# Linear attention into a gated MLP on one core: batch 1's loads, norms and turn rearranged

## The chip, the cores and the metric

The kernel runs on one core of one Trainium2 chip. The metric is the time of one execution on the device in microseconds, as the median over several runs.

## What is computed

Attention without a score matrix: q is normed over the head dimension, k over the sequence, and a 64 x 64 product of k and v per head takes the place of the scores. Its output, 4608 tokens by 512, goes through an MLP with hidden width 2048 and the activation h * sigmoid(beta * h).

```python
q_s = exp(q - max(q, -1));  q_s = q_s / (sum(q_s, -1) + 1e-9)      # q, k, v: (8, 8, 576, 64)
k_s = exp(k - max(k, 2));   k_s = k_s / (sum(k_s, 2) + 1e-9)
kv  = einsum('bhsd,bhse->bhde', k_s, v)
x   = einsum('bhsd,bhde->bhse', q_s, kv).transpose(0, 2, 1, 3).reshape(4608, 512)
h   = x @ w_in                                                      # 512 -> 2048
out = (h * (1 / (1 + exp(-beta * h)))) @ w_out                      # 2048 -> 512
```

Inputs and output are float32; products run in bfloat16.

## The kernel before

**Tiling.** The tokens are cut into nine slabs of 512: slab t below 8 holds the first 512 positions of batch t, slab 8 the last 64 of each batch. A slab has two passes. Pass 1 makes the hidden layer transposed, 16 tiles of 128 hidden rows (`pass1_tile`, index f), each of four 128x128 by 128x512 products (index m, one for each pair of heads) into one PSUM bank, then one Silu on ACT into `GT` (L648). Pass 2 (`pass2_group`) multiplies `GT` by `WOUT` into four output tiles (index u) of 16 products each. A product of both passes is one 128x512 matmul; PE has one line for all of them, L372, and L370 for transposes.

**The attention part** works on pairs of heads (hp 0 to 3). `exp_q` (L314, ACT) makes `EQ` from `QF`. `norm_main` (L331) sums each row (L338, DVE), takes the reciprocal (L339, DVE) and multiplies (L340, on DVE or on GpSimd, named POOL). For batch 1, `t_steps` transposes the normed pairs on PE (L370) and copies them to `QT` (L391, ACT). `exp_kc` (L322, ACT) and `cast_v` (L357) prepare k and v; `kv_half` multiplies them for two pairs (36 small products) and scales the result into `KVC` (L441 and L443, DVE); `out_half` makes two pairs of `XT`, the input of pass 1, by four products of 64x64 by 64x512 and a copy from PSUM for each pair (`out_evac`, L459).

**The weights.** `load_wout` brings float32 rows of W_out into staging buffers, which are the ones that W_in came through: rows 8 to 11 go into `O2S[1]`, as soon as DVE has cast the W_in that lay there. `scale_wout` (L562, DVE) scales one row block f with 1/beta into `WOUT`. A product of pass 2 with index f needs row block f.

**What sets the order.** Each engine works through its own queue in the order in which the program adds the operations, and `add` derives the waits from what an operation reads and writes, PSUM banks included. All loads below are issued by SP, in program order. The order around the first turn, from slab 0 to slab 1, is written out by hand. In pass 2 of slab 0, f is the outer loop and all four u run side by side in banks 3 to 6; for f of 14 and 15, u = 0 and 1 come first. Before pass 2 stand, for DVE, `scale_wout` and the norms of batch 1 (L795 to L808). Inside it, `todo` (L756) inserts batch 1's work after given products: `slot` starts at 64, so an entry of 104 comes after product 40 of the 64. Bank numbers of slab 0's and slab 1's tiles come from `HFIRST` (L652); beyond its end, slab 1 takes banks 0, 1, 2 in turn. `FIRST` (L669) says how many tiles of a slab are begun at the turn, with the m loop outside, so that products with m = 0 and 1 can run before pairs 2 and 3 of `XT` are there (`by_m`, L657). `o2_evac` (L702) copies an output tile from PSUM to `O2S` for the store.

**Loads of batch 1's q.** `load_swapped` (L272) has four loads x of 256 KB, two heads each: x = 0 is pair 0, x = 1 is pair 2, and x = 2 and x = 3 are the even and the odd heads of pairs 1 and 3 together. So pairs 1 and 3 need both x = 2 and x = 3.

Of the kernel before, what the change touches and what calls it, by code (L numbers as in the profile page):

```python
# [7 lines left out]
ACT = mybir.ActivationFunctionType  # L8
# [35 lines left out]
class Program:  # L44
# [12 lines left out]
    def add(self, eng, fn, r=(), w=(), bank=(), slot=None, after=()):  # L57
        op = Op(eng, fn, slot)
        op.pos = len(self.ops)
        deps = op.deps  # L60
        deps.extend(after)
        for k in r:
            deps.extend(self.writer.get(k, ()))
            self.readers.setdefault(k, []).append(op)
        for k in w:
            for d in self.readers.get(k, ()):
                if d is not op and not self._same(d, op):
                    deps.append(d)
            for d in self.writer.get(k, ()):
                if not self._same(d, op):  # L70
                    deps.append(d)
            self.readers[k] = []
            self.writer[k] = [op]
        for k in bank:
            t = self.touch.setdefault(k, {})
            for e, d in t.items():
                if e != eng:
                    deps.append(d)
            t[eng] = op
        if eng == POOL and slot is None:  # L80
            if self.pool is not None:
                deps.append(self.pool)
            self.pool = op
        self.ops.append(op)
        return op
# [78 lines left out]
def bass_efficient_attn_shen__then__act_swish_beta_kernel(  # L164
# [12 lines left out]
    with ExitStack() as es:  # L177
# [36 lines left out]
        WARM = sb("WARM", [128, 512], BF16)  # L214
# [57 lines left out]
        def load_swapped(b, xs=range(4)):  # L272
            i = b % 2
            for x in xs:
                s0, d0, n = SLOTS[x]
                a = bass.AP(qt_h, (b * H + s0) * S * D,
                            [[4 * D, 128], [n * S * D, 2], [1, 4 * D]])
                o = bass.AP(QF[i], d0 * 4 * D, [[H * 4 * D, 128], [n * 4 * D, 2], [1, 4 * D]])
                add(SP, lambda e, o=o, a=a: e.dma_start(o, a),
                    w=[("qf", i, hp, x) for hp in ((0,), (2,), (1, 3), (1, 3))[x]],  # L280
                    slot=f"qs{i}{x}")
# [173 lines left out]
        def out_evac(b, bks, hps=range(NHP)):  # L455
            i = b % 2
            for hp in hps:
                eng, bk = (ACTE if hp % 2 else DVE), bks[hp]
                add(eng, lambda e, eng=eng, bk=bk, hp=hp: (  # L459
                    e.copy if eng == ACTE else e.tensor_copy)(XT[i][:, hp, :], PS[bk][:, :]),  # L460
                    r=[("ps", bk)], w=[("xt", i, hp)], bank=[bk])
# [19 lines left out]
        def kv_half(b, bks, a):  # L481
            kv_prods(b, bks, (a,))
            kv_evac(b, bks, (a,))

        def out_half(b, bks, a):
            out_prods(b, bks, (a,))
            out_evac(b, bks, (a, a + 1))
# [53 lines left out]
        def go(steps):  # L541
            for s in steps:
                s()
# [105 lines left out]
                                                 scale=BETA[:, f:f + 1]),  # L649
                    r=[("ps", bk), "beta"], w=[("gt", f)], bank=[bk])  # L650

        HFIRST = ((3, 4, 5, 6, 0, 1, 7, 2, 3, 4, 5, 6, 0, 1, 7, 2), (1, 3, 2, 4, 5, 6, 0, 7))  # L652

        def hbank(t, f):
            return HFIRST[t][f] if t < 2 and f < len(HFIRST[t]) else HB[f % 3]
# [10 lines left out]
                pass1_mm(t, f, m, bk)  # L666
                tick()

        FIRST = (16, 5)  # L669
        at = by_m(0, 0, 4)  # L670
        at(0)
        out_now(0, 3, 7, DVE)
# [14 lines left out]
                at(m)  # L687
        load_wout(0)
        load_wout(4)
        load_swapped(1, (0, 2))  # L690
        load_wout(8)
        load_swapped(1, (3, 1))
        load_k(1, 4, (0, 1))
        load_wout(12, 2)
        load_v(1, 4, (0, 1))
# [51 lines left out]
        for t in range(NSLAB):  # L747
            todo = []
            if t == 0:
                def evacs():  # L750
                    o2_evac(0, 0, 3, DVE)
                    o2_evac(0, 1, 4, ACTE)
                    add(ACTE, lambda e: e.activation(DUMMY[:, 2:3], WARM[:, 0:1], ACT.Silu),
                        r=["warm"], w=["dummy"])

                todo = [(104, lambda: go(t_steps(1, (0, 1), (1,), ACTE))),  # L756
                        (104.1, lambda: cast_v(1, 0, ACTE)),
                        (109, lambda: go(t_steps(1, (2, 3), (2,), ACTE))),
                        (109.1, lambda: (scale_wout(14, 2), exp_kc(1, 2), exp_kc(1, 3))),
                        (115, lambda: kv_half(1, (7, 0), 0)),  # L760
                        (122, lambda: out_half(1, (1, 2), 0)), (124.5, evacs),
                        (127, lambda: kv_half(1, (7, 0), 2))]
            elif t == 1:
                todo = [(103, lambda: (kv_prods(2, (1, 2), (0, 2)), kv_evac(2, (1, 2)))),
                        (118, lambda: block(2))]
            elif t < 7:
                todo = [(104, lambda: block(t + 1))]
            todo = sorted(todo, key=lambda x: -x[0])
            slot = [0]

            def tick():
                slot[0] += 1
                while todo and todo[-1][0] <= slot[0]:
                    todo.pop()[1]()

            if 2 <= t < 7:
                if t < 5:
                    load(t + 2 if t == 2 else t + 3)
                for hp in (0, 2):
                    norm_main(t + 1, hp, 2)  # L780
                    t_dma(t + 1, hp, 2)
                if t in (2, 3, 4, 6):
                    norm_rem(t // 2 if t != 3 else 0)
                    tr_dma(t // 2 if t != 3 else 0)
                if t == 2:
                    load(5)
            elif t == 1:
                for hp in range(NHP):
                    cast_v(2, hp)
            if t < 2:  # L790
                slot[0] = NM * FIRST[t]
            for f in range(FIRST[t] if t < 2 else 0, NF):
                pass1_tile(t, f, tick)
            if t == 0:
                load(2)  # L795
                scale_wout(0)
                scale_wout(4)
                exp_q(1, (0,))
                norm_main(1, 0, 1)
                scale_wout(8)  # L800
                exp_q(1, (1, 3, 2))
                norm_main(1, 1, 1, POOL)
                norm_main(1, 3, 1, POOL)
                norm_main(1, 2, 1)
                exp_kc(1, 0, 2)
                scale_wout(12, 2)
                for hp in range(1, NHP):
                    cast_v(1, hp)  # L808
                pass2_group(0, (0, 1, 2, 3), (3, 4, 5, 6), tick)
                while todo:  # L810
                    todo.pop()[1]()
                at = by_m(1, 0, FIRST[1])
                o2_evac(0, 2, 5, ACTE)
                at(0, 0, 3)
                at(1, 0, 3)
                out_half(1, (7, 7, 7, 0), 2)
                o2_evac(0, 3, 6, DVE)
                at(0, 3)
                at(1, 3)
                at(2)  # L820
                at(3)
                store(0)
                load(3)
                load_qrem(0)
                continue
            nb = [t + 2] if t + 2 < B else []
            if t == 1:
                nb = [2, 3]
            late = []
            for b in nb:  # L830
                if t == 1 and b == 2:
                    exp_q(2)
                    for hp in range(2):
                        norm_main(2, hp, 1, POOL)
                    t_dma(2, 0, 2)
                for hp in (0, 2):
                    exp_kc(b, hp, 2)
                if b > 2:
                    late.append(b)
                if b > 3:  # L840
                    for hp in range(NHP):
                        cast_v(b, hp)
            for b in late:
                exp_q(b)
                if b % 2 == 1:
                    exp_qr(b // 2)
                if b == 3:
                    exp_qr(0)
            for u in range(4):
                if (t, u) == (8, 3):  # L850
                    last_tile(u, ((0, 384), (384, 512)), (OB[orot[0] % 2], MB[0]))
                    continue
                pass2_group(t, (u,), (OB[orot[0] % 2],), tick)
                orot[0] += 1
                if t == 1 and u == 0:
                    for hp in range(2, 4):
                        norm_main(2, hp, 1, POOL if hp == 2 else DVE)
                    t_dma(2, 2, 2)
                    for hp in range(NHP):
                        cast_v(3, hp)  # L860
            while todo:
                todo.pop()[1]()
            if t < 8:
                store(t)
# [30 lines left out]
```

## Time and profile before

| | |
|---|---|
| median of 9 runs | 280.62 us (280.43 to 282.29) |
| the profiled execution | 280.53 us |
| its span, first to last instruction | 278.7 us |
| granted TensorE clock | 1.000 |
| PE busy in the span | 270.1 us (97%) |
| ACT, DVE, POOL busy | 166.8, 102.6, 33.5 us |
| a Silu (L648) | 689 ns, 144 of them |
| GpSimd's norm multiply (L340) of one pair | 1042 ns, 8 of them |
| pass 2 of slab 0 and the turn to slab 1 | about 28 to 48 us of the span |

Rows of a timeline read: start in us from the span's start, duration in us, engine, line of the kernel, operation, output tile <- input tiles, shape, how many merged; in brackets the idle time of the engine before the row and what ended it. PEld is the weight load of a matmul. A few per cent of the matmul records are missing, so a count of 5 may stand for 6. In a group line, the numbers after the bar are busy us and mean ns of one, then the idle time before.

### The profile page before, as it was taken

What the parts mean: (1) busy time and instruction counts of PE and PEld (TensorE: products, weight loads), DVE (VectorE), ACT (ScalarE), POOL (GpSimd) and SP (SyncE); (2) the same over time, 40 slices, a digit from 0 to 9 for tenths busy, and PEclk for the clock granted to TensorE, in tenths of its full rate; (3) what the DMA queues carried; (4) which work ended last, traced back from release to release, by engine and by line L of the source; (5) the groups of instructions that cost most, each with busy time, mean ns of one, the idle gap of its engine ahead of it and who ended that gap; (6) DMA issues with size and microseconds to landing.
All of it is one profiled execution on the core that took longest, in us unless ns stands there. A gap on an engine that the chain in (4) does not pass through costs nothing.

```text
span 278.7 us, 4595 instructions
## 1 busy us (share of the span) xinstructions
PE 270.1 (97%) x1899; PEld 131.0 (47%) x1929; DVE 102.6 (37%) x206; ACT 166.8 (60%) x240; POOL 33.5 (12%) x50
## 2 busy tenths in 40 slices
PE   7899989999999999999999999999999999999995
PEld 3545444444445454545454545444444444444443
DVE  4744785008590149205730462035603300110012
ACT  4868476889578736793579437853751175027500
POOL 2630041307000304030002000000000000000000
DMA  7999999997089799960599133002600120011022
GB/s 228 385 387 401 388 390 377 393 374 136 17 290 368 201 341 281 388 133 2 153 383 209 33 150 75 2 4 94 151 0 2 58 93 2 0 75 75 2 73 78
DMA packets 42174, 50.12 MB, mean 180 GB/s; under 512 B 21029, under 2 KB 29477, under 8 KB 41001
## 3 DMA queue, kind: packets, MB, share of 16 engines
q1 hardware_dynamic: 41312, 48.90, 54.3%
q10 hardware_dynamic: 840, 0.93, 1.1%
q8 instruction: 15, 0.25, 0.4%
q14 instruction: 7, 0.05, 0.0%
HBM read 36.71 MB, written 9.44 MB: 166 GB/s over the span
## 4 chain that ended last, share of the span: by engine, by line
PE 84%; DMA 8%; SPq 4%; DVE 2%; issue 1%
PE PS L372 84%; DMA O2S<-in_moe_w_out_dram 4%; DMA O2S<-in_moe_w_in_dram 4%; SPq L569 2%; SPq L250 1%; DVE QS L338 1%; DVE WOUT L562 1%; DVE EQ L340 0%; SPq L293 0%; DVE WIN L573 0%; PE PS L370 0%; DVE QI L339 0%; SPq L298 0%; DVE O2S L724 0%
## 5 line engine op out<-in xcount | busy, mean ns | idle before, releaser
L648 ACT ACTIVATE GT<-PS,BETA 128x512 bf16<-128x512 f32 x144 | 96.8, 689 | 61.6 <-PE PS L372 61.6
L372 PE MATMUL PS<-WOUT,GT 128*128 128x512 bf16 (+2 forms) x573 | 125.2, 373 | 1.8 <-issue 1.3
L372 PE MATMUL PS<-XT,WIN 128*128 128x512 bf16 x566 | 125.6, 379 | 0.8 <-issue 0.3
L372 PEld LDWEIGHTS PS<-XT,WIN 128*128 128x128 bf16 x576 | 60.4, 106 | 63.6 <-issue 0.4
L372 PEld LDWEIGHTS PS<-WOUT,GT 128*128 128x128 bf16 x592 | 56.6, 98 | 65.8 <-issue 1.1
L703 DVE COPY O2S<-PS 128x512 f32<-128x512 f32 x33 | 22.7, 688 | 124.3 <-PE PS L372 124.3
L357 POOL CAST VB<-VF 128x576 bf16<-128x576 f32 x29 | 21.2, 730 | 85.6 <-DMA VF<-in_v_dram 84.3
L338 DVE TENSOR_REDUCE QS<-EQ 128x8 f32<-128x512 bf16 (+1 forms) x22 | 20.0, 910 | 17.3 <-ACT EQ L314 17.3
L459 ACT CAST XT<-PS 128x512 bf16<-128x512 f32 x14 | 7.6, 587 | 23.2 <-PE PS L372 23.2
L322 ACT ACTIVATE EK<-KF 128x1152 bf16<-128x1152 f32 (+1 forms) x19 | 18.4, 1005 | 3.2 <-DMA KF<-in_k_dram 2.9
L314 ACT ACTIVATE EQ<-QF 128x512 bf16<-128x512 f32 x32 | 17.6, 615 | 4.3 <-DMA QF<-in_q_dram 4.3
L340 DVE TENSOR_TENSOR EQ<-EQ,QI 128x1024 bf16<-128x1024 bf16 (+1 forms) x14 | 16.2, 1156 | 0.5
L459 DVE CAST XT<-PS 128x512 bf16<-128x512 f32 x14 | 9.1, 686 | 13.4 <-PE PS L372 13.4
L340 POOL TENSOR_TENSOR EQ<-EQ,QI 128x512 bf16<-128x512 bf16 x8 | 8.3, 1042 | 32.8 <-DVE QI L339 32.4
L372 PEld LDWEIGHTS PS<-VB,EK 64*64 64x64 bf16 x576 | 6.6, 107 | 5.0 <-issue 2.5
L372 PE MATMUL PS<-VB,EK 64*64 64x65 bf16 x576 | 8.0, 193 | 0.8 <-ACT VB L357 0.4
L648 ACT ACT_TABLE_LOAD x5 | 6.4, 1283 | 0.1
L372 PE MATMUL PS<-QT,KVC 64*64 64x512 bf16 x64 | 6.2, 383 | 0.0
L372 PE MATMUL PS<-XT 128*128 128x512 f32 x6 | 4.4, 887 | 1.5 <-DVE XT L226 1.5
L339 DVE RECIPROCAL QI<-QS 128x8 f32<-128x8 f32 (+1 forms) x22 | 5.0, 226 | 0.8
L322 ACT ACT_TABLE_LOAD x4 | 5.1, 1283 | 0.1
L443 DVE TENSOR_TENSOR KVC<-PS,RC 128x128 bf16<-128x128 f32 (+1 forms) x16 | 4.4, 274 | 0.6
(51 smaller groups left out, 66.9 us busy)
## 6 DMA issues: line engine op xcount, KB each, us to landing
out_dram<-O2S SPq DMA_DIRECT2D x8, 1024.0 KB, 4.6
QF<-in_q_dram SPq DMA_DIRECT2D x30, 256.0 KB, 6.0
KF<-in_k_dram SPq DMA_DIRECT2D x6, 1152.0 KB, 8.4
VF<-in_v_dram SPq DMA_DIRECT2D x6, 1152.0 KB, 11.7
KF<-in_k_dram SPq DMA_DIRECT2D x8, 288.0 KB, 8.2
VF<-in_v_dram SPq DMA_DIRECT2D x8, 288.0 KB, 8.5
WST<-in_moe_w_in_dram SPq DMA_DIRECT2D x8, 256.0 KB, 7.4
O2S<-in_moe_w_in_dram SPq DMA_DIRECT2D x4, 512.0 KB, 10.8
```

The source lines that it names most:

```text
L314: add(ACTE, lambda e, o=o, a=a: e.activation(o, a, ACT.Exp), r=[("qf", i, hp, x) for x in ((2, 3) if hp % 2 else (hp // 2,))], w=[("eq", i ...
L322: add(ACTE, lambda e: e.activation(o, a, ACT.Exp), r=[("kf", i, h) for h in range(hp, hp + n)], w=[("ekc", i, h) for h in range(hp, hp + n)])
L338: add(DVE, lambda e: e.tensor_reduce(s_, a, AX.X, ALU.add), r=ks, w=[("qs", i, hp0)])
L339: add(DVE, lambda e: e.reciprocal(v_, s_), r=[("qs", i, hp0)], w=[("qi", i, hp0)])
L340: add(eng, lambda e: e.tensor_tensor(a, a, vb, ALU.mult), r=ks + [("qi", i, hp0)], w=ks)
L357: add(eng, lambda e: (e.copy if eng == ACTE else e.tensor_copy)(o, a), r=[("vf", i, hp), ("vone", i)], w=[("vb", i, hp, h) for h in ((0, 1 ...
L372: add(PE, lambda e: e.matmul(o, l, r_, start=start, stop=stop, tile_position=tp), r=r, w=w, bank=[bk])
L443: add(DVE, lambda e, o=o, p_=p_, vb=vb: e.tensor_tensor(o, p_, vb, ALU.mult), r=[("ps", bk)] + [("rc", i, hp) for hp in hps], w=[("kvc", k ...
L459: add(eng, lambda e, eng=eng, bk=bk, hp=hp: (e.copy if eng == ACTE else e.tensor_copy)(XT[i][:, hp, :], PS[bk][:, :]), r=[("ps", bk)], w=[ ...
L569: add(SP, lambda e: e.dma_start(STAGE[c][:, m:m + nm, :], a), w=SKEY[c][m:m + nm], slot=f"win{c}{m}")
L648: add(ACTE, lambda e: e.activation(GT[:, f, :], PS[bk][:, :], ACT.Silu, scale=BETA[:, f:f + 1]), r=[("ps", bk), "beta"], w=[("gt", f)], ba ...
L703: add(eng, lambda e: (e.copy if eng == ACTE else e.tensor_copy)(O2S[t % 2][:, u, :], PS[bk][:, :]), r=[("ps", bk)], w=[("o2", t % 2, u)], ...
```

## The change

All of it concerns batch 1 at the turn from slab 0 to slab 1:

- load x = 3 of batch 1's q is issued ahead of W_out rows 8 to 11, not behind them;
- the norm of pair 0 multiplies on GpSimd, not on DVE, and `scale_wout(8)` is cut in two: rows 8 and 9 before pair 1's norm, rows 10 and 11 after it;
- the entries of `todo` move: transposes of pairs 0 and 1 from after product 40 to after 42, of pairs 2 and 3 from 45 to 49, the first kv half from 51 to 53, the first output half from 58 to 59;
- the second kv half, which stood before product 64, stands behind six products of slab 1 (three tiles, m = 0 and 1); the second output half, which stood there, stands behind six more;
- slab 1 begins six tiles at the turn, not five, and takes all eight banks for its 16 tiles;
- the copy of output tile u = 3 and the activation that loads the Silu table are added before slab 1's first products; the table's load stands behind the copy of tile u = 2, not before it;
- in the second output half of batch 1, ACT copies pair 2 and DVE pair 3, where it was the other way round.

```diff
-                eng, bk = (ACTE if hp % 2 else DVE), bks[hp]
+                eng, bk = (ACTE if (hp % 2) != (b == 1 and hp > 1) else DVE), bks[hp]
...
-        HFIRST = ((3, 4, 5, 6, 0, 1, 7, 2, 3, 4, 5, 6, 0, 1, 7, 2), (1, 3, 2, 4, 5, 6, 0, 7))
+        HFIRST = ((3, 4, 5, 6, 0, 1, 7, 2, 3, 4, 5, 6, 0, 1, 7, 2), (1, 3, 2, 4, 5, 6, 7, 0, 1, 3, 2, 4, 5, 6, 7, 0))
...
-        FIRST = (16, 5)
+        FIRST = (16, 6)
...
-        load_swapped(1, (0, 2))
+        load_swapped(1, (0, 2, 3))
         load_wout(8)
-        load_swapped(1, (3, 1))
+        load_swapped(1, (1,))
...
                     o2_evac(0, 0, 3, DVE)
                     o2_evac(0, 1, 4, ACTE)
-                    add(ACTE, lambda e: e.activation(DUMMY[:, 2:3], WARM[:, 0:1], ACT.Silu),
-                        r=["warm"], w=["dummy"])
-
-                todo = [(104, lambda: go(t_steps(1, (0, 1), (1,), ACTE))),
-                        (104.1, lambda: cast_v(1, 0, ACTE)),
-                        (109, lambda: go(t_steps(1, (2, 3), (2,), ACTE))),
-                        (109.1, lambda: (scale_wout(14, 2), exp_kc(1, 2), exp_kc(1, 3))),
-                        (115, lambda: kv_half(1, (7, 0), 0)),
-                        (122, lambda: out_half(1, (1, 2), 0)), (124.5, evacs),
-                        (127, lambda: kv_half(1, (7, 0), 2))]
+
+                todo = [(106, lambda: go(t_steps(1, (0, 1), (1,), ACTE))),
+                        (106.1, lambda: cast_v(1, 0, ACTE)),
+                        (113, lambda: go(t_steps(1, (2, 3), (2,), ACTE))),
+                        (113.1, lambda: (scale_wout(14, 2), exp_kc(1, 2), exp_kc(1, 3))),
+                        (117, lambda: kv_half(1, (7, 0), 0)),
+                        (123, lambda: out_half(1, (1, 2), 0)), (124.5, evacs)]
...
-                norm_main(1, 0, 1)
-                scale_wout(8)
+                norm_main(1, 0, 1, POOL)
+                scale_wout(8, 2)
                 exp_q(1, (1, 3, 2))
                 norm_main(1, 1, 1, POOL)
+                scale_wout(10, 2)
                 norm_main(1, 3, 1, POOL)
                 norm_main(1, 2, 1)
...
                 o2_evac(0, 2, 5, ACTE)
+                o2_evac(0, 3, 6, DVE)
+                add(ACTE, lambda e: e.activation(DUMMY[:, 2:3], WARM[:, 0:1], ACT.Silu),
+                    r=["warm"], w=["dummy"])
                 at(0, 0, 3)
                 at(1, 0, 3)
-                out_half(1, (7, 7, 7, 0), 2)
-                o2_evac(0, 3, 6, DVE)
+                kv_half(1, (7, 0), 2)
                 at(0, 3)
                 at(1, 3)
+                out_half(1, (7, 7, 7, 0), 2)
                 at(2)
                 at(3)
```

## The prediction

> **What bounds the kernel now.** The page first: PE is busy for 97% of the span, and the chain of work that ended last is PE for 84%.
>
> ```profile
> PE 270.1 (97%) x1899; PEld 131.0 (47%) x1929; DVE 102.6 (37%) x206; ACT 166.8 (60%) x240; POOL 33.5 (12%) x50
> PE 84%; DMA 8%; SPq 4%; DVE 2%; issue 1%
> ```
>
> So the change pays only where PE waits, and whatever PE loses goes onto the end: in order of time the chain of waits is PE without a break from 39.27 us on, and its long pieces start at 226.07, 236.86, 247.66, 258.45 us, 50 products every 10.79 us (0.216 us each; one record in 50 is missing). Next, PE's timeline where slab 0 turns into slab 1:
>
> ```profile
> 36.80 0.39 PE L370 MATMUL PS<-IDB,EQ 128*128 128x128 bf16 x4
> 37.60 0.40 PE L370 MATMUL PS<-IDB,EQ 128*128 128x128 bf16 x4 [0.42 <-POOL EQ L340]
> 37.84 1.24 PE L372 MATMUL PS<-WOUT,GT 128*128 128x512 bf16 x5
> 39.27 0.62 PE L370 MATMUL PS<-IDB,EQ 128*128 128x128 bf16 x8 [0.19 <-DVE EQ L340]
> 39.73 1.46 PE L372 MATMUL PS<-WOUT,GT 128*128 128x512 bf16 x6
> ...
> 46.78 0.41 PE L372 MATMUL PS<-QT,KVC 64*64 64x512 bf16 x4
> 47.12 12.82 PE L372 MATMUL PS<-XT,WIN 128*128 128x512 bf16 x57
> ```
>
> See two waits. Pair 1's transposes could start at 37.02 and start at 37.60: 0.58 us. After five products (38.92) pairs 3 and 2 start at 39.27: 0.35. Two more are too short for these rows: in its single instructions, pair 3's share of the second kv half waits 0.09 us for GpSimd's cast, and at 53.7 us PE waits for a bank whose Silu was late (58 products from 47.12 to 59.78 are 12.66 us, 12.53 at the rate: 0.13). Together 1.15 us: all that can be won. Then DVE, which makes what PE waits for, and its neighbours:
>
> ```profile
> 32.36 0.69 DVE L340 TENSOR_TENSOR EQ<-EQ,QI 128x512 bf16<-128x512 bf16 x1
> 33.92 1.67 DVE L562 TENSOR_SCALAR WOUT<-O2S,RB 128x512 bf16<-128x512 f32 x4 [0.87 <-DMA O2S<-in_moe_w_out_dram]
> 35.51 0.68 DVE L338 TENSOR_REDUCE QS<-EQ 128x8 f32<-128x512 bf16 x1
> 36.22 0.20 DVE L339 RECIPROCAL QI<-QS 128x8 f32<-128x8 f32 x1
> 36.34 0.63 DVE L338 TENSOR_REDUCE QS<-EQ 128x8 f32<-128x512 bf16 x1
> ...
> 38.03 1.18 DVE L340 TENSOR_TENSOR EQ<-EQ,QI 128x512 bf16<-128x512 bf16 x1
> 39.14 0.87 DVE L562 TENSOR_SCALAR WOUT<-O2S,RB 128x512 bf16<-128x512 f32 x2
> 40.28 1.16 DVE L562 TENSOR_SCALAR WOUT<-O2S,RB 128x512 bf16<-128x512 f32 x2 [0.28 <-DMA O2S<-in_moe_w_out_dram]
> ```
> ```profile
> 36.50 2.16 POOL L340 TENSOR_TENSOR EQ<-EQ,QI 128x512 bf16<-128x512 bf16 x2 [19.30 <-DVE QI L339]
> 39.63 0.90 POOL L357 CAST VB<-VF 128x576 bf16<-128x576 f32 x1 [0.97 <-DMA VF<-in_v_dram]
> 42.50 0.67 POOL L357 CAST VB<-VF 128x576 bf16<-128x576 f32 x1 [1.97 <-DMA VF<-in_v_dram]
> ```
> ```profile
> 34.68 1.67 ACT L314 ACTIVATE EQ<-QF 128x512 bf16<-128x512 f32 x3 [3.32 <-DMA QF<-in_q_dram]
> 47.27 0.59 ACT L459 CAST XT<-PS 128x512 bf16<-128x512 f32 x1 [0.42 <-PE PS L372]
> ```
>
> From 33.92 to 39.14 DVE never rests: its start is the landing of W_out rows 8 to 11, its end is row 12's scaling. And DVE and GpSimd hinder each other. The multiply (L340) takes 0.69 us alone, 1.18 beside GpSimd's, ending (39.21) 0.55 after GpSimd's end (38.66). GpSimd's cast takes 0.67 alone and 0.90 where it starts during a scaling, ending (40.53) 0.52 after that scaling (40.01); the next scaling, started at 40.28, ends (40.81) 0.28 after the cast.
>
> [...] The trace agrees: the three endings above, and the reduces of 0.63 to 0.68 us beside GpSimd's multiply. [...] The trace agrees: the waits for loads end in the order of issue.
>
> **Part 1, one load sooner.** Load x=3 (odd heads of pairs 1 and 3) goes ahead of W_out 8. Before, W_out 8 was there for DVE at 33.92 and x=3 for ACT at 34.68, so x=3 takes about 0.70 us (256 KB at the 389 GB/s of that window are 0.67). W_out 8 was issued at 22.71 and landed 11 us later, behind a full queue; so it now lands 0.70 later, DVE starts row 8 at 34.62. SP has time for the issue (its wait before 22.71). ACT's exponentials of pairs 1 and 3 come 2.6 us sooner, hidden: DVE's reduces stand behind rows 8 and 9. Loads after x=3 land as before.
>
> **Part 2, the norms.** Pair 0's multiply goes to GpSimd at 32.4, done by 33.45, under free time. DVE is then at: row 8 34.62, row 9 35.02 (0.40 apart: 1.59 us for four), reduce of pair 1 35.42, reciprocal 36.13 (0.71), row 10 36.25 (0.12), to end at 36.73. GpSimd asks for pair 1's multiply at 36.41 (0.28 after the reciprocal's start, as at 36.22 and 36.50). [...] GpSimd, asking before row 11's start at 36.65, gets it: ends 36.73 + 0.90 (1.04[...]) = 37.63. Row 11 ends 0.28 later, 37.91. The reverse, [...] no row shows; row 11 would end at 37.13. [...] Then reduce of pair 3 37.83, reciprocal 38.54, reduce of pair 2 38.66, reciprocal 39.33 (0.67), multiply 39.57 (0.24). GpSimd's pair 3 runs 38.82 to 39.86, so DVE's multiply ends 0.55 later, 40.41. GpSimd's cast of pair 1's v (landed by 39.63) asks at 39.93, before row 12's start at 40.33, so it goes first, to 40.93, and row 12 ends at 41.21. Before: 39.61.
>
> **PE against it.** Before, product 40 starts at 36.58. Now 41 and 42 follow, at 0.1 us late for row 8, then the transposes of pairs 0 and 1, the latter at 37.69, done at 37.92, hidden by what follows; products 43 to 48 to 39.21. Product 49 needs row 12: 41.21 + 0.06 = 41.27, a wait of 2.06 us. Queued behind it are pairs 3 and 2's transposes and all of PE. Product 50 starts at 41.27 + 0.22 + 0.46 + 0.03 = 41.98, with the same work done as before at 40.59 (39.73 + 4 x 0.216). **+1.39**; the waits of 0.58 and 0.35 are within this difference.
>
> **Part 3, the turn's end.** (a) Output half 0 now stands before product 60, and the second kv half no longer stands between it and slab 1. Bank 3 is emptied by DVE (L703) behind XT pair 0's copy. Before: outputs at 43.14, that copy 43.59, O2S 44.20 to 44.88, that is 1.74 after the outputs, ready for PE at 1.79. Slab 1's second product wants bank 3 after 0.34 + 0.01 + 6 x 0.216 = 1.65. **+0.17** with a slow restart of 0.03. (b) The kv half behind six products finds its casts done: **-0.09**. (c) Outputs of pairs 2 and 3 stand directly before the six m=2 products, which read XT pair 2. Before, four products lay between: outputs at 46.78, DVE's copy done at 47.91, m=2 just in time. Now ACT copies pair 2: start 0.49 after the outputs (47.27), 0.57 to 0.59 long, PE 0.06 later: 1.11, and PE's outputs take 0.34 (46.78 to 47.12): 0.77, with restart **+0.80** (0.70 to 0.90). Pair 3 on DVE hides under m=2. (d) Eight banks for slab 1 in place of three from tile 8 on: **-0.13**. (e) The Silu table load (1.28 us) moves behind `o2_evac(0, 2)`; ACT is free from about 46.8 to the copy, so it costs 0. The sixth first tile adds no work. The store of slab 0 goes sooner into a DMA that is no longer awaited: 0.
>
> **Sum.** 1.39 + 0.17 - 0.09 + 0.80 - 0.13 = +2.14 us on the profiled execution's 280.53 (span 278.7, 1.83 around it): 282.67. The median of the nine runs is 0.09 higher, so I say **282.7**.
>
> **Rivals.** (A) [...] row 12 is ahead of the cast. Row 11 ends 37.13, GpSimd's pair 1 38.03, pair 3 39.13, DVE's multiply 39.68, row 12 40.08: product 50 at 40.84, +0.25 for +1.39, sum +1.00: 281.5. For: DVE's queue is gapless at its starts[...]. (B) W_out 8 lands no later, since x=3 shares the engines: all of part 2 is 0.70 sooner, +1.44: 282.0. Against: the order of the waits. (C) Not slower: the waits of PE go and none takes their place at row 12. Place: product 49; price: each us by which row 12 ends after 39.15 (PE's own 39.21). Product 50 would then start at 39.92, -0.67; with a pair-1 norm that isn't held up, -0.81. The sum is +0.08 to -0.06: about 280.5. It decides if row 12 ends before 39.15, 2.1 us sooner than I find; GpSimd's taking over of pair 0 speaks for it, the later start at 34.62 against it. Even then (c) eats the gain.
>
> **Chances.** Forecast 0.60 (own range 282.2 to 283.0; the low end is the cast coming after row 12, which ends at 40.81), A 0.25 (281.3 to 281.8), B 0.06, C 0.09. Some 0.3%, 0.84 us, is what a measurement can tell from no change. Slower by more: the forecast, B and over half of A, 0.80; within it 0.17; faster 0.03. The range reaches to A: 281.4 to 283.0.
>
> **What would show it.** Right: row 8 starting at 34.6; a GpSimd multiply ending about 0.9 after row 10, with row 11 some 1.2 us long; PE waiting about 2 us for DVE WOUT after product 48, 0.8 for ACT XT in front of m=2; no wait at 53.7. Wrong: row 11 of 0.48 us (A), row 8 at 33.9 (B), no PE wait for WOUT (C), or a PE wait elsewhere after slab 1 starts.

## The result and the profile after

The changed kernel takes 282.26 us (median of 10 runs, 281.62 to 284.47) against 280.65 us: the ratio is 1.0064, 95% interval 1.0048 to 1.0079, that is 1.3 to 2.2 us slower. Its profiled execution took 282.34 us (span 280.5), 1.81 more than that of before. The longest execution, 284.47 us, ran at a granted clock of 0.994, and so did five of the nine of e4 below, four of which took 283.0 to 283.9 us.

The start of an execution varies, and PE and the loads vary apart from each other: among the fourteen profiles of this study pass 2 of slab 0 begins between 27.95 and 29.56 us, and the scaling of row 0, which waits for an earlier load of W_out, between 26.73 and 28.77. So within a profile, PE's times are taken from product 40 (the 40th of slab 0's 64 in pass 2; product 49 is the first with f = 12) and DVE's from row 0 or row 8. Here product 40 stands at 36.45 us (37.10 less three products), before at 36.58.

PE's timeline of the changed kernel at the turn:

```profile
37.10 0.71 PE L370 MATMUL PS<-IDB,EQ 128*128 128x128 bf16 x8
37.64 1.46 PE L372 MATMUL PS<-WOUT,GT 128*128 128x512 bf16 x6
41.06 0.39 PE L372 MATMUL PS<-WOUT,GT 128*128 128x512 bf16 x1 [1.96 <-DVE WOUT L562]
41.29 0.61 PE L370 MATMUL PS<-IDB,EQ 128*128 128x128 bf16 x8
41.73 1.03 PE L372 MATMUL PS<-WOUT,GT 128*128 128x512 bf16 x4
...
45.93 1.61 PE L372 MATMUL PS<-XT,WIN 128*128 128x512 bf16 x6
...
49.29 0.41 PE L372 MATMUL PS<-QT,KVC 64*64 64x512 bf16 x4
50.38 1.90 PE L372 MATMUL PS<-XT,WIN 128*128 128x512 bf16 x8 [0.68 <-ACT XT L459]
```

The two waits in front of the transposes are gone: all eight of pairs 0 and 1 run at once, all eight of pairs 3 and 2 too. In their place stands one wait of 1.96 us in front of product 49, for row 12 of W_out. Six products of slab 1 take 1.61 us where they took 1.46 before: bank 3. And from the output half to the first m = 2 product it is 1.09 us, where the four small products need 0.34: XT pair 2.

DVE and GpSimd in the same stretch:

```profile
34.39 0.88 DVE L562 TENSOR_SCALAR WOUT<-O2S,RB 128x512 bf16<-128x512 f32 x2 [2.25 <-DMA O2S<-in_moe_w_out_dram]
...
36.02 1.62 DVE L562 TENSOR_SCALAR WOUT<-O2S,RB 128x512 bf16<-128x512 f32 x2
...
39.29 0.91 DVE L340 TENSOR_TENSOR EQ<-EQ,QI 128x512 bf16<-128x512 bf16 x1
40.12 2.07 DVE L562 TENSOR_SCALAR WOUT<-O2S,RB 128x512 bf16<-128x512 f32 x4
```
```profile
36.24 1.11 POOL L340 TENSOR_TENSOR EQ<-EQ,QI 128x512 bf16<-128x512 bf16 x1 [2.99 <-DVE QI L339]
38.61 1.04 POOL L340 TENSOR_TENSOR EQ<-EQ,QI 128x512 bf16<-128x512 bf16 x1 [1.26 <-DVE QI L339]
39.78 0.94 POOL L357 CAST VB<-VF 128x576 bf16<-128x576 f32 x1
```

Rows 8 and 9 take 0.88 us together, rows 10 and 11 take 1.62. In the single instructions row 10 ends at 36.45, GpSimd's multiply 0.90 later at 37.35, and row 11, started at 36.37, 0.28 after that: it is 1.27 us long. DVE's multiply of pair 2 ends (40.20) 0.55 after GpSimd's of pair 3 (39.65), the cast (40.72) 0.52 after DVE's multiply, row 12 (41.00) 0.28 after the cast, and PE starts product 49 at 41.06. It is a chain of five handovers between the two engines. The 0.28, 0.55 and 0.52 are the lengths that the prediction read from the profile before; its 0.90 was an estimate, the 1.04 us of GpSimd's multiply less 0.14, as 0.55 is DVE's 0.69 less 0.14. The traces show the turns and their lengths, not what makes the two engines take them.

The sum from product 40 on: product 50 comes 5.28 us after it, 4.01 before (+1.27); bank 3 +0.16; XT pair 2 +0.75; less 0.09 for the cast and 0.13 for the bank at 53.7 us, both of which are no longer waited for: +1.96. Read directly, slab 1's pass 2 begins 25.16 us after product 40 (61.61), before 23.20 (59.78): +1.96 too. Product 40 came 0.13 earlier here, which leaves 1.83, and the profiled executions differ by 1.81.

### The profile page after: what moved, and what is told of

Read it like the earlier page. It is cut to its first block, busy times and chain, and to the rows that moved or that the text cites. A ratio compares the mean times of both kernels' runs of the same rounds, so it can differ in the third digit from the quotient of the medians.

```text
span 280.5 us, 4594 instructions
## 1 busy us (share of the span) xinstructions
PE 270.5 (96%) x1899; PEld 131.3 (47%) x1929; DVE 103.2 (37%) x205; ACT 166.6 (59%) x240; POOL 34.2 (12%) x51
## 4 chain that ended last, share of the span: by engine, by line
PE 83%; DMA 8%; SPq 4%; DVE 2%; issue 1%; ACT 0%
PE PS L372 83%; DMA O2S<-in_moe_w_out_dram 4%; DMA O2S<-in_moe_w_in_dram 4%; SPq L569 2%; SPq L250 2%; DVE WOUT L562 1%; DVE QS L338 1%; SPq L293 0%; DVE EQ L340 0%; DVE QI L339 0%; ACT XT L459 0%; SPq L298 0%; PE PS L370 0%; DVE O2S L724 0%
## 5 line engine op out<-in xcount | busy, mean ns | idle before, releaser
L372 PE MATMUL PS<-WOUT,GT 128*128 128x512 bf16 (+2 forms) x574 | 125.4, 373 | 3.7 <-DVE WOUT L562 2.0
L372 PE MATMUL PS<-XT,WIN 128*128 128x512 bf16 x565 | 125.6, 379 | 1.5 <-ACT XT L459 0.7
L372 PEld LDWEIGHTS PS<-XT,WIN 128*128 128x128 bf16 x576 | 60.5, 106 | 64.2 <-ACT XT L459 1.0
L372 PEld LDWEIGHTS PS<-WOUT,GT 128*128 128x128 bf16 x592 | 56.4, 98 | 68.4 <-DVE WOUT L562 3.0
L459 ACT CAST XT<-PS 128x512 bf16<-128x512 f32 x14 | 7.6, 588 | 25.3 <-PE PS L372 25.3
L340 DVE TENSOR_TENSOR EQ<-EQ,QI 128x1024 bf16<-128x1024 bf16 (+1 forms) x13 | 15.2, 1169 | 0.5
L459 DVE CAST XT<-PS 128x512 bf16<-128x512 f32 x14 | 9.1, 686 | 13.0 <-PE PS L372 13.0
L340 POOL TENSOR_TENSOR EQ<-EQ,QI 128x512 bf16<-128x512 bf16 x9 | 9.4, 1049 | 35.2 <-DVE QI L339 35.0
L372 PEld LDWEIGHTS PS<-VB,EK 64*64 64x64 bf16 x576 | 6.5, 107 | 4.3 <-issue 3.2
L372 PE MATMUL PS<-VB,EK 64*64 64x65 bf16 x576 | 7.9, 193 | 0.5 <-POOL VB L357 0.2
L372 PE MATMUL PS<-XT 128*128 128x512 f32 x6 | 5.3, 1054 | 1.5 <-DVE XT L226 1.5
L372 PE MATMUL PS<-QT,KVC 64*64 64x512 bf16 x64 | 6.2, 383 | 0.0
L562 DVE TENSOR_SCALAR WOUT<-O2S,RB 128x512 bf16<-128x512 f32 x8 | 4.6, 621 | 2.3 <-DMA O2S<-in_moe_w_out_dram 2.3
```

The costliest lines, as they stand in the source:

```text
L340: add(eng, lambda e: e.tensor_tensor(a, a, vb, ALU.mult), r=ks + [("qi", i, hp0)], w=ks)
L372: add(PE, lambda e: e.matmul(o, l, r_, start=start, stop=stop, tile_position=tp), r=r, w=w, bank=[bk])
L459: add(eng, lambda e, eng=eng, bk=bk, hp=hp: (e.copy if eng == ACTE else e.tensor_copy)(XT[i][:, hp, :], PS[bk][:, :]), r=[("ps", bk)], w=[ ...
L562: add(DVE, lambda e, f=f: e.tensor_scalar(WOUT[:, f, :], STAGE[f // 4][:, f % 4, :], RB[:, f:f + 1], None, ALU.mult), r=[SKEY[f // 4][f % ...
```

## Experiments

Theory: PE's wait for row 12 is made by DVE and GpSimd taking turns (row 11, 1.27 us long, behind pair 1's multiply; row 12, 0.88 us, behind the cast), on top of DVE's later start at row 8; the output half without cover costs another 0.75 us. Rivals: DVE's queue is long by its number of instructions and what GpSimd does beside it is no matter; the later load is the whole cost; the two parts only hurt together.

**e1: the load back behind W_out 8, in the changed kernel.**

```diff
-        load_swapped(1, (0, 2, 3))
+        load_swapped(1, (0, 2))
         load_wout(8)
-        load_swapped(1, (1,))
+        load_swapped(1, (3, 1))
```

> The changed kernel with load x=3 behind W_out 8 to 11 again. [...] row 8 starts 0.67 us sooner (about 33.7), but DVE then waits at pair 1's reduce for the exponential, which needs x=3; that reduce starts about 0.1 us sooner than in the changed kernel, and so does all that follows: 282.1 to 282.3. Rival, that the later load itself cost its 0.67 us: 281.6.

282.50 us (6 runs, 282.15 to 284.68), ratio to before 1.0078 (1.0052 to 1.0103): no gain, and 0.2 to 0.4 us more than expected. In its profile (the longest of its runs) row 8 comes 6.80 us after row 0, 7.40 in the changed kernel, but DVE then waits at pair 1's reduce for the exponential, and PE waits 1.96 us for row 12, as in the changed kernel:

```profile
35.97 0.69 DVE L338 TENSOR_REDUCE QS<-EQ 128x8 f32<-128x512 bf16 x1 [0.60 <-ACT EQ L314]
```

The load cannot be undone by itself: with the new order on DVE, x=3 is needed that soon.

**e2: rows 8 to 11 together again, in the changed kernel.**

```diff
-                scale_wout(8, 2)
+                scale_wout(8)
                 exp_q(1, (1, 3, 2))
                 norm_main(1, 1, 1, POOL)
-                scale_wout(10, 2)
```

> The changed kernel with rows 8 to 11 scaled together before pair 1's norm; DVE has the same instructions, in another order. [...] row 11 is back at 0.48 us instead of 1.27, GpSimd's multiply of pair 1 ends about 38.0 beside reduces alone; the cast of pair 1's v still stands before row 12, which ends about 40.5 instead of 41.0: 0.5 us less than the changed kernel, 281.7. Rival, that DVE's chain is long by its number of instructions: no difference, 282.3.

282.30 us (5 runs, 281.90 to 283.25), ratio 1.0051 (1.0037 to 1.0066). The median shows no gain; the ratio is 0.0013 under that of the change (0.36 us), within both intervals. So the time alone does not decide, and the profile has to. DVE, then GpSimd:

```profile
35.77 1.68 DVE L562 TENSOR_SCALAR WOUT<-O2S,RB 128x512 bf16<-128x512 f32 x4 [2.31 <-DMA O2S<-in_moe_w_out_dram]
...
39.89 1.24 DVE L340 TENSOR_TENSOR EQ<-EQ,QI 128x512 bf16<-128x512 bf16 x1
41.06 2.06 DVE L562 TENSOR_SCALAR WOUT<-O2S,RB 128x512 bf16<-128x512 f32 x4
```
```profile
38.42 2.16 POOL L340 TENSOR_TENSOR EQ<-EQ,QI 128x512 bf16<-128x512 bf16 x2 [3.83 <-DVE QI L339]
40.76 0.90 POOL L357 CAST VB<-VF 128x576 bf16<-128x576 f32 x1 [0.17 <-DMA VF<-in_v_dram]
```

The four rows take 1.68 us, none is held up. Row 12 now ends 6.17 us after row 8's start (41.94), in the changed kernel 6.62: 0.45 less with the same instructions on the same engines. So it is where GpSimd's multiply falls among DVE's instructions, not their count. PE keeps the gain: slab 1's pass 2 begins 24.71 us after product 40, in the changed kernel 25.16. (Pair 1's transposes now wait 0.65 us for GpSimd's multiply, which PE would otherwise have waited in front of product 49.) The profiled execution is the longest of the five, and both its pass 2 (29.21) and its row 0 (28.39) are late, so the time of the whole hides what the turn gains. The rest of the conflict stays, as forecast: DVE's multiply of pair 2 waits for GpSimd's of pair 3 (1.24 us) and row 12 for the cast (41.06 to 41.94).

**e3: the cast of pair 1's v on ACT, in the changed kernel.**

```diff
-                        (106.1, lambda: cast_v(1, 0, ACTE)),
+                        (106.1, lambda: (cast_v(1, 0, ACTE), cast_v(1, 1, ACTE))),
...
-                for hp in range(1, NHP):
+                for hp in range(2, NHP):
                     cast_v(1, hp)
```

> The changed kernel with the cast of pair 1's v on ACT. [...] nothing stands between DVE's multiply of pair 2 and row 12, which takes 0.48 instead of 0.88 us; PE's wait for row 12 falls from 1.96 to about 1.55 us: 281.9. Rival, that row 12 is long for another reason (PE or the DMAs reading beside it): no difference, 282.3.

281.98 us (6 runs, 281.66 to 282.96), ratio 1.0048 (1.0032 to 1.0063). The intervals overlap here too, and the profile decides:

```profile
35.40 0.88 DVE L562 TENSOR_SCALAR WOUT<-O2S,RB 128x512 bf16<-128x512 f32 x2 [2.23 <-DMA O2S<-in_moe_w_out_dram]
...
41.14 1.66 DVE L562 TENSOR_SCALAR WOUT<-O2S,RB 128x512 bf16<-128x512 f32 x4
```

Rows 12 to 15 take 1.66 us where they took 2.07, and row 12 ends 6.21 us after row 8's start instead of 6.62. As forecast: row 12 was long because of the cast. Slab 1's pass 2 begins 24.76 us after product 40, 0.4 us sooner than in the changed kernel.

**e4: the same products at the turn's end, with cover for the copies.**

```diff
                 at(0, 0, 3)
-                at(1, 0, 3)
                 kv_half(1, (7, 0), 2)
-                at(0, 3)
-                at(1, 3)
+                at(1, 0, 3)
+                at(0, 3, 5)
                 out_half(1, (7, 7, 7, 0), 2)
+                at(0, 5)
+                at(1, 3)
                 at(2)
```

> The changed kernel with the same products in another order at the turn's end: three of slab 1, second kv half, five, second output half, four, then m = 2. Theory that the uncovered copy of XT pair 2 costs 0.74 us: this wait goes, 281.5. Rival, that PE then waits elsewhere (for KVC in front of the output half): 282.2.

281.85 us (9 runs, 281.49 to 283.88), ratio 1.0065 (1.0042 to 1.0088): by the ratio no gain on the changed kernel. Without the four longest executions the median is 281.61, but that choice was made after seeing them, so again the profile has to decide. PE's timeline:

```profile
41.16 0.39 PE L372 MATMUL PS<-WOUT,GT 128*128 128x512 bf16 x1 [0.78 <-DVE WOUT L562]
...
48.52 0.41 PE L372 MATMUL PS<-QT,KVC 64*64 64x512 bf16 x4
48.87 3.41 PE L372 MATMUL PS<-XT,WIN 128*128 128x512 bf16 x15
```

From the output half PE goes on after 0.35 us and runs through to m = 2: the wait of 0.75 is gone and none takes its place. From row 12's end to slab 1's pass 2 it takes 19.87 us (41.10 to 60.97), in the changed kernel 20.61 (41.00 to 61.61): 0.74 less. In this execution pass 2 began at 29.41 us instead of 27.98, but row 8 at 34.30, and so its wait for row 12 is only 0.78 us: row 12 hangs on the load, and here PE's late start cost next to nothing (product 49 at 41.16, in the changed kernel at 41.06).

**e5 and e6: each part alone, on the kernel before.** e5 has the turn's end alone, with its six tiles, eight banks, the engines of the two copies and the place of the table load; e6 has the loads, the norms and the positions in pass 2, with the second kv half before product 64 as it was.

e5:

```diff
-                        (122, lambda: out_half(1, (1, 2), 0)), (124.5, evacs),
-                        (127, lambda: kv_half(1, (7, 0), 2))]
+                        (122, lambda: out_half(1, (1, 2), 0)), (124.5, evacs)]
...
                 at(1, 0, 3)
-                out_half(1, (7, 7, 7, 0), 2)
-                o2_evac(0, 3, 6, DVE)
+                kv_half(1, (7, 0), 2)
                 at(0, 3)
                 at(1, 3)
+                out_half(1, (7, 7, 7, 0), 2)
```

e6:

```diff
-                norm_main(1, 0, 1)
-                scale_wout(8)
+                norm_main(1, 0, 1, POOL)
+                scale_wout(8, 2)
                 exp_q(1, (1, 3, 2))
                 norm_main(1, 1, 1, POOL)
+                scale_wout(10, 2)
```

> The kernel before with the turn's end of the change alone (second kv half behind six products of slab 1, output half behind six more, six tiles, eight banks, ACT on pair 2, table load moved). Theory of the uncovered copy: +0.75 for XT pair 2 in front of m = 2, -0.09 and -0.13 for the cast and the bank that are no longer waited for; bank 3 isn't waited for, since the output half stands one product earlier than in the change. Sum +0.5: 281.1. Rival, that the turn's end gains what it was made for and the loss is all in the norms: 280.4.

> The kernel before with the loads, the norms and the positions in pass 2 of the change, but the turn's end as before (second kv half before product 64). Theory: the row-12 wait of about 2 us comes in place of 0.58 and 0.35, +1.3 at product 50, and the kv half no longer waits for its cast, -0.09: 281.8. Rival, that both parts only hurt together: 280.6.

e5: 280.90 us (21 runs) against 280.48, ratio 1.0013 (1.0005 to 1.0020), +0.4 where 0.5 was expected. e6: 281.76 us (5 runs), ratio 1.0044 (1.0030 to 1.0059), +1.3 as expected. Their lines for PE, e5 first:

```profile
48.81 3.41 PE L372 MATMUL PS<-XT,WIN 128*128 128x512 bf16 x15 [0.68 <-ACT XT L459]
```
```profile
41.25 0.39 PE L372 MATMUL PS<-WOUT,GT 128*128 128x512 bf16 x1 [1.79 <-DVE WOUT L562]
```

Each wait comes with its own part. The two losses, 0.42 and 1.28, add up to 1.70, and the change lost 1.6 by the medians, 1.8 by the ratio: they do not need each other, and neither part gains on the whole.

**f1: the order of the loads alone, on the kernel before** (the two changed load lines of the change and nothing else).

> The kernel before with the order of the loads of the change alone: x=3 ahead of W_out 8 to 11. Theory: DVE's chain from row 8 to pair 2's multiply is shifted by 0.67 us as a whole, and PE's wait for pairs 3 and 2 with it: 281.1 to 281.2. Rival, that the sooner exponentials pay: 280.5 or less.

280.99 us (22 runs) against 280.54, ratio 1.0017 (1.0010 to 1.0024): +0.5. In its profile row 8 starts 7.43 us after row 0 (34.16 and 26.73), 6.74 before (33.92 and 27.18), and nothing uses the sooner exponentials. PE feels only a part of this 0.69 here: pair 1's transposes wait 0.82 us instead of 0.58, and product 50 comes 0.24 later after product 40, since the loads of this execution ran 0.46 us further ahead of PE than in the profile before (row 0 stood 1.44 us before pass 2, there 0.98). The load is a cost of its own, somewhat less than the 0.6 expected.

**f2: pair 0's multiply back on DVE, in the changed kernel** (`norm_main(1, 0, 1)` for `norm_main(1, 0, 1, POOL)`).

> The changed kernel with pair 0's multiply on DVE as before. Theory: its 0.69 us lie in the 2.2 us in which DVE waits for W_out 8, so no difference: 282.3. Rival, that the move to GpSimd gained its 0.69 us: 282.9.

282.39 us (5 runs, 282.33 to 282.45), ratio 1.0061 (1.0046 to 1.0077): no difference, and slab 1's pass 2 begins 25.16 us after product 40, as in the changed kernel. What GpSimd takes over here was under DVE's wait of 2.25 us for W_out 8.

**e7 and e8: what the freed time is good for.** With x=3 there at 31.8 us, DVE can norm pair 1 by itself before row 8 comes. e7 does that; e8 also lays the turn's end in fours and changes slab 1's second and third bank.

e7, in the changed kernel:

```diff
                 norm_main(1, 0, 1, POOL)
-                scale_wout(8, 2)
                 exp_q(1, (1, 3, 2))
-                norm_main(1, 1, 1, POOL)
-                scale_wout(10, 2)
+                norm_main(1, 1, 1)
+                scale_wout(8)
                 norm_main(1, 3, 1, POOL)
                 norm_main(1, 2, 1)
```

e8, with that; slab 1's banks begin with 1, 2, 3, 4 and not 1, 3, 2, 4:

```diff
                 at(0, 0, 3)
-                at(1, 0, 3)
+                at(1, 0, 1)
                 kv_half(1, (7, 0), 2)
-                at(0, 3)
-                at(1, 3)
+                at(1, 1, 3)
+                at(0, 3, 5)
                 out_half(1, (7, 7, 7, 0), 2)
+                at(0, 5)
+                at(1, 3)
                 at(2)
```

> The changed kernel with pair 1's norm wholly on DVE ahead of rows 8 to 11, in the 2.2 us in which DVE waits for them; rows 8 to 11 together; pairs 3 and 2 after them. No GpSimd instruction stands between row 8 and row 11. [...] row 12 ends about 2.0 us sooner against row 8's start than in the changed kernel (4.6 instead of 6.6 us), PE's wait for it falls under 0.3 us: 280.2. Rival, that PE then waits as long for another input of the turn (v's cast or k's exponential of pairs 2 and 3, whose loads land as before): 281 or more.

> As the one before, and with it the turn's end in fours: four products of slab 1, second kv half, four, second output half, four, then m = 2; slab 1's second tile takes bank 2 and its third bank 3. Theory: 0.74 for XT pair 2 and 0.16 for bank 3 go as well: 279.4, about 0.4% below the kernel before. Rival, that the loads of v and k of pairs 2 and 3, which land at 43 to 44 us, are waited for now: 280.0 to 280.4.

e7: 280.78 us (14 runs, 280.31 to 281.51), ratio 1.0011 (1.0000 to 1.0022). DVE in its profile:

```profile
34.99 1.66 DVE L562 TENSOR_SCALAR WOUT<-O2S,RB 128x512 bf16<-128x512 f32 x4
...
39.14 0.87 DVE L562 TENSOR_SCALAR WOUT<-O2S,RB 128x512 bf16<-128x512 f32 x2
```

Row 12 ends 4.63 us after row 8's start, as expected, and in this execution PE does not wait for it. 1.5 us of the 2.0 expected are there in the time. Two reasons can be given for the rest, and how much each accounts for isn't shown. This execution entered pass 2 at 29.25 us and reached product 49 at 40.06, after row 12 (39.62); one that enters pass 2 at 28.16 would be there at 38.97 and wait some 0.7 us (an estimate). And with no wait at row 12 a late start is no longer hidden: the fourteen runs fall into eight of 280.31 to 280.83 us and six of 281.26 to 281.51, and the profiled one, which started late, is one of the six (281.37).

e8: 279.80 us (22 runs, 279.44 to 280.91) against 280.48, ratio 0.9979 (0.9969 to 0.9990): faster than both kernels, though only by 0.6 us (by the ratio) where 1.1 was expected. In its profile no wait of PE for XT pair 2 or bank 3 is left; one of some 0.24 us for row 12 is, inside this row, where seven products at 0.216 us would take 1.67:

```profile
38.41 1.92 PE L372 MATMUL PS<-WOUT,GT 128*128 128x512 bf16 x7
```

Slab 1's pass 2 begins 22.31 us after product 40, in the two profiles of the kernel before (f4 has the second) 23.20 and 22.95. This execution entered pass 2 at 28.89 us, 0.7 to 0.9 later than those two, which takes about as much back.

**f3: rows 12 and 13 ahead of pair 2's multiply, on e8.** `norm_main` gets a step between the reciprocal and the multiply, in which `scale_wout(12, 2)` stands; the transposes of pairs 2 and 3 come after product 53.

> The kernel with early norm and the turn in fours, in which rows 12 and 13 are scaled ahead of pair 2's multiply and the transposes of pairs 2 and 3 come after product 53. Theory: where PE reaches product 49 before row 12 is there (it does where it starts pass 2 at about 28 us), it no longer waits, 0.4 us less: 279.4. Rival, that the transposes or the kv half now wait for pair 2's multiply as long: 279.8.

279.71 us (22 runs, 279.40 to 281.24), ratio 0.9974 (0.9965 to 0.9983): not to be told from e8. PE's timeline at slab 1's first products (L374 and L461 are L372 and L459, two lines further down):

```profile
45.87 0.82 PE L374 MATMUL PS<-XT,WIN 128*128 128x512 bf16 x3 [0.17 <-ACT XT L461]
```

From product 43 to 53 PE no longer waits (39.17 to 41.54 us, eleven products at 0.216). But slab 1's second product now waits 0.33 us (0.17 beyond the end of the one before) for the bank that ACT's copy of XT pair 1 empties. Here what was gained at one place is given back at the next. This execution entered pass 2 at 29.56 us; how others divide is not shown.

**f4: the kernel before once more.**

> The kernel before once more, for a second profile of it: if the start (pass 2 of slab 0 from 27.9 to 29.4 us in the other profiles) varies from execution to execution and not with the kernel, its pass 2 may start anywhere in that stretch, and its time is that of before, 280.5.

280.43 us (21 runs); pass 2 from 27.97 us, row 8 from 33.51. Its loads are further ahead of PE than in the first profile (row 0 stands 1.11 us before pass 2 and not 0.98), pair 1's transposes wait 0.21 us less, and the way from product 40 to slab 1's pass 2 is 0.25 us shorter: that much the kernel before varies by itself. In eight of the fourteen profiles pass 2 starts at 28.48 us or later, in neither of the two of the kernel before; the changed kernel, e5, f1 and f2 start at 27.95 to 28.17 as well. So it isn't the order of the loads alone. Whether the start depends on the kernel at all stays open.

## Why the prediction was right, point by point

The forecast was 282.7 us, measured 282.26: slower, by the waits it named, some 0.4 us less than forecast.

- **The load.** Forecast 0.70 us later for W_out 8. Row 8 started at 34.39 with pass 2 0.18 earlier than before: 0.65. From row 0 to row 8 it takes 6.65 to 6.80 us in the four profiles with the old order (before, e1, e5, f4) and 7.24 to 7.43 in those with the new one, e7 apart, where DVE itself is late at row 8 (7.71). Alone it costs 0.5 us (f1); within the change it is the price of the sooner exponentials, which pair 1's reduce needs once it stands behind two rows of W_out instead of four (e1), and that sooner reduce won nothing: with the four rows in front of it again, row 12 comes 0.45 us sooner (e2).
- **Who goes first.** This was the step that decided between the forecast and rival A, in which row 11 ends ahead of GpSimd's multiply of pair 1. The profile before showed neither: that GpSimd goes between was the author's assumption. Here its multiply starts at 36.24 us, while row 10 runs and before row 11 starts (36.37), and ends at 37.35, 0.28 before row 11, which is 1.27 us long: it went between two DVE instructions that stand back to back. e2 takes that away and row 12 comes 0.45 us sooner, e3 takes the handovers at the cast away, 0.41. Rival A, row 11 of 0.48 us, is out. Rival B is out by row 8's start.
- **Product 50.** Forecast +1.39, measured +1.27 from product 40. Row 12 ended 4.55 us after product 40, forecast 4.63; PE then needed 0.73 us to product 50, forecast 0.77.
- **The turn's end.** Bank 3 +0.16 for +0.17; XT pair 2 +0.75 for +0.80 (the restart of 0.03 in both forecasts is an estimate: in the profile before, four transposes take 0.24 us after a wait, 37.60 to 37.84, and 0.22 without one, 36.80 to 37.02); the cast and the late bank gone, -0.09 and -0.13 as forecast; the table load (46.57 to 47.85) is over before the copy at 49.74 and cost nothing. e4 and e5 show the turn with and without cover for the copy: 0.74 us less in e4's profile, 0.4 us more in e5's time.
- **Pair 0 on GpSimd** at nothing: f2. It isn't free in every execution: in e4's profile this multiply still ran when row 8 started (34.30) and ended at 34.68, and row 8 took 0.66 us instead of 0.48.
- **The sum.** +2.14 forecast, +1.96 from product 40 on: 0.12 of the difference at product 50, the rest at the turn's end. What then remains lies before the change's reach: the profiled execution entered pass 2 0.18 us sooner. The sum had taken the start of the one profile of before as given, and with row 12 tied to a load, a shift between PE and the loads goes into PE's wait. That the terms agree to a tenth of a us is in part luck: both profiles have row 0 at 0.98 to 0.99 us before pass 2. In e4's, where it is 2.48, the wait for row 12 was 0.78 us, and compared with f4's profile of before the change costs 2.21 from product 40 on.
- **Rival C** asked for row 12 before 39.15 us. It needs GpSimd out of the way and pair 1's norm ahead of row 8, which e7 and e8 do.

## What to carry to other kernels

When work goes from DVE to GpSimd to relieve DVE, lay both queues side by side in time: here a multiply on GpSimd between two scalings on DVE made the second one 1.27 us long instead of 0.48, and its consumers waited with it. Look first at what the engine is waiting for: here DVE had 2.25 us of waiting for a load, and moving pair 1's norm into it (e7) won back 1.5 us of the change's loss (e7 also takes GpSimd's multiply from between the scalings), where moving pair 0's multiply out of it won nothing (f2). And when products are rearranged around a PSUM copy, count the products between the producer and the first reader of the copy: this one needed, by the prediction's estimate, some 0.77 us of other products; with none PE stood for 0.75 us, and with four, 0.86 us of work, not at all (e4).

## What the runs showed that was not expected

A wait on a load can hide a late start of PE: e4's execution entered pass 2 1.4 us late and waited 1.2 us less at row 12. It hides nothing where the loads are late as well: in the profiles of e2 and e3 row 0 stood 1.4 and 1.1 us later than in the changed kernel's, and these two are the longest executions of their runs. And a DVE instruction that is held up by GpSimd shows here as a long instruction, not as idle time: the group of these scalings has a mean of 621 ns in the changed kernel,

```profile
L562 DVE TENSOR_SCALAR WOUT<-O2S,RB 128x512 bf16<-128x512 f32 x8 | 4.6, 621 | 2.3 <-DMA O2S<-in_moe_w_out_dram 2.3
```

where each takes 0.48 us alone: two waits for GpSimd, of row 11 (1.27 us) and row 12 (0.88), are hidden in a busy time.
